# Batch 1's queries repacked by GpSimd and turned in 16 full transposes, with its second K^T V half and second scores one pair of products later

## Chip, cores, metric

One Trainium2 (trn2) chip, one core of it. The metric is the device time of one execution in microseconds (us); lower is better. Time before: 284.09 us, median of three runs (283.82 to 284.26).

## The reference, cut to what matters

```python
# q, k, v: [8 batches, 8 heads, 576 rows, 64]; w_in [512, 2048]; w_out [2048, 512]
kv  = einsum('bhsd,bhse->bhde', k, v)          # K^T V, one 64x64 matrix per head
out = einsum('bhsd,bhde->bhse', q, kv)         # "scores" below
x   = out / sqrt(mean(out**2, -1) + 1e-6) * g_norm
h   = x.reshape(4608, 512) @ w_in              # first product
y   = elu(h) @ w_out                           # second product
```

The kernel works in bf16 with float32 sums. It takes 512 rows of each batch in turn, and the 64 left over of each batch as a ninth group. TensorE writes its results to PSUM, its output memory; ACT and VectorE copy them from there to SBUF, where TensorE reads its operands. Such a copy is called an eviction here.

## The kernel before

The order of instructions on each engine is the order in the program. Batch 0 is done first. While its second product runs, TensorE also makes batch 1 ready: it transposes batch 1's q, forms K^T V and the scores in two halves `u`, and transposes the normalised rows, a half at a time.

```python
def q_t_single(q_pk, qt_ps, r, p):             # two 64-column transposes per 128 rows
    for j in range(J):
        for l in range(2):
            nc.tensor.transpose(
                qt_ps[l * 64 : l * 64 + 64, r, j * P : j * P + P],
                q_pk[:, 2 * p + l, j, :],
                ident,
            )

def q_t():
    qt_ps = at_tile(BF16).rearrange("p (r t) -> p r t", r=NPAIR)   # PSUM tile "at", one buffer
    ...
    for p in range(NPAIR):
        q_t_single(raw["q", T], qt_ps, p, p)
    nc.scalar.copy(qT[:, 0:2, :], qt_ps[:, 0:2, :])
    nc.scalar.copy(qT[:, 2:4, :], qt_ps[:, 2:4, :])
...
load_w_out(10, 12)                             # GpSimd issues these transfers
load_w_out(12, 14)
load_w_out(14, FC)
...
for j in range(J):
    mm2_quarter(0, j, 0)                       # second product of batch 0, rows 0..3 of w_out
    if j == 2:
        at["q"]()
for j in range(J):
    mm2_quarter(0, j, 1)
    if j == 1:
        at["kvu0"]()                           # first K^T V half
    if j == 2:
        at["seu0"](scores)                     # first scores, then square and sum
        at["sq0"]()
        at["sum0"]()
at["inv0"]()
at["mulu0"]()
for j in range(J):
    mm2(0, j, 8, 10)
    if j == 2:
        at["kvu1"]()                           # second K^T V half
at["seu1"]()                                   # second scores
at["sq1"]()
at["sum1"]()
for j in range(J):
    mm2(0, j, 10, 12)                          # rows 10 and 11 of w_out
    if j == 1:
        at["inv1"]()
        at["xu0"](scores[:, 0, :])             # first transposes of normalised rows
at["mulu1"]()
...
for j in range(J):
    mm2(0, j, 12, 14)
for j in range(J):
    mm2(0, j, 14, FC, hold=j > 1)
    if j == 0:
        at["xu1"](scores[:, 1, :])             # second transposes of normalised rows
```

`mm2(0, j, f0, f1)` issues one product of 128x512 for each row block `f` of w_out ("row" means such a block of 128). After this stretch the first product of batch 1 begins.

## Time and profile before

Two moments of TensorE: **S**, the start of batch 0's second product, and **E**, the start of batch 1's first product. What lies before S is called the head, and what lies between the first product on rows 10 and 11 and E the tail.

| kernel before, first trace | us |
|---|---|
| S | 28.31 |
| rows 10 and 11 of w_out land | 39.84 |
| first product on them starts | 39.97 |
| E | 46.06 |
| E - S, "the stretch" | 17.75 |

S and E are read from TensorE's timeline of the kernel before; columns are start, duration of the group, engine, source line, operation, output and inputs, shapes, count.

```profile
28.31 2.75 PE L514 MATMUL o_ps<-w_out_sb,gT 128*128 128x512 bf16 x12
...
39.63 0.41 PE L373 MATMUL at<-kv_sb,qT 64*128 64x64 bf16 x16
39.97 1.04 PE L514 MATMUL o_ps<-w_out_sb,gT 128*128 128x512 bf16 x4
...
46.06 1.89 PE L467 MATMUL at<-xT,w_in_sb 128*128 128x512 bf16 x8
```

From E on, TensorE is the bound, and each microsecond by which E moves is a microsecond of the result unless something later adds to it.

### The profile page before, as it was taken

Reading aid. Unit: us, or ns where it says so; the run is one execution under the profiler, and the core shown is the slowest. Engines: PE = TensorE matmul, PEld = TensorE weight load, DVE = VectorE, ACT = ScalarE, POOL = GpSimd, SP = SyncE. Lnnn points to the kernel's source line nnn. Section 1 sums busy time; section 2 is a strip of 40 time slices with the busy share of each in tenths; the row PEclk is TensorE's granted clock in tenths of the full one; section 3 lists DMA queues with packets and bytes.
Section 4 is the critical chain, followed back from the end, with each engine's and each line's share of the span. In section 5 each row is a group of like instructions: output and inputs, shape, how many; then the busy total and the mean of one; then the engine's idle time right before and its main releaser. Section 6 shows DMA issues by size and latency. Waiting matters only on the chain.

```text
span 282.0 us, 5163 instructions
## 1 busy us (share of the span) xinstructions
PE 276.0 (98%) x2134; PEld 129.8 (46%) x2134; DVE 159.8 (57%) x232; ACT 153.8 (55%) x221; POOL 56.2 (20%) x98
## 2 busy tenths in 40 slices
PE   7899999999999999999999999999999999999994
PEld 3444544445444444444444444444444444444444
DVE  2559453888388546843693469445854586444400
ACT  2679546666487438533863377337923692333311
POOL 7854422143421341004110421012000000000000
PEclk9999999999999999999999999999999999999999
DMA  7999999697796696359935795455236123010122
GB/s 196 199 200 202 208 201 191 179 170 128 178 177 114 157 157 156 74 149 121 198 78 148 95 211 73 130 114 148 55 94 76 77 38 112 0 77 0 74 76 74
DMA packets 57579, 35.98 MB, mean 128 GB/s; under 512 B 32852, under 2 KB 55124, under 8 KB 57556
## 3 DMA queue, kind: packets, MB, share of 16 engines
q0 software_dynamic: 21808, 17.30, 41.2%
q1 hardware_dynamic: 35348, 17.83, 24.7%
q10 hardware_dynamic: 400, 0.52, 0.6%
q8 instruction: 16, 0.26, 0.4%
q14 instruction: 7, 0.06, 0.1%
HBM read 36.70 MB, written 9.44 MB: 164 GB/s over the span
## 4 chain that ended last, share of the span: by engine, by line
PE 94%; DMA 2%; ACT 1%; DVE 0%; issue 0%; POOL 0%; POOLq 0%
PE h_ps L467 42%; PE o_ps L514 39%; PE o_ps L924 5%; DMA v_pk<-in_v_dram 2%; PE at L174 2%; PE at L467 1%; PE bank L684 1%; PE at L201 1%; PE h_ps L684 1%; PE se_ps L201 1%; ACT r L669 0%; ACT r L672 0%; PE at L185 0%; ACT sq L663 0%; PE se_ps L413 0%
## 5 line engine op out<-in xcount | busy, mean ns | idle before, releaser
L467 PE MATMUL h_ps<-xT,w_in_sb 128*128 128x512 bf16 x536 | 125.7, 379 | 0.0
L514 PE MATMUL o_ps<-w_out_sb,gT 128*128 128x512 bf16 x512 | 120.5, 379 | 0.0
L479 ACT ACTIVATE elu_e<-h_ps 128x1024 bf16<-128x1024 f32 (+1 forms) x71 | 70.0, 995 | 80.1 <-PE h_ps L467 78.5
L467 PEld LDWEIGHTS <-w_in_sb 128*128 128x128 bf16 x552 | 52.5, 98 | 63.3 <-DVE xT L333 1.7
L514 PEld LDWEIGHTS <-gT 128*128 128x128 bf16 x512 | 49.4, 98 | 58.4
L490 DVE TENSOR_SCALAR elu_e<-elu_e 128x1024 bf16<-128x1024 bf16 (+1 forms) x75 | 31.9, 425 | 73.4 <-ACT elu_e L479 73.4
L498 DVE TENSOR_TENSOR gT<-elu_e,h_ps 128x1024 bf16<-128x1024 bf16 (+1 forms) x51 | 60.1, 1179 | 5.3
L527 ACT COPY o_sb<-o_ps 128x512 f32<-128x512 f32 x32 | 18.6, 586 | 15.5 <-PE o_ps L514 15.5
L218 DVE TENSOR_REDUCE ss<-sq 128x16 f32<-128x1024 bf16 x16 | 19.4, 1218 | 11.1 <-ACT sq L213 10.4
L485 ACT ACTIVATE elu_h<-h_ps 128x1024 bf16<-128x1024 f32 (+1 forms) x20 | 19.5, 990 | 0.0
L150 POOL COPY q_bf<-q_pk 128x512 bf16<-128x512 bf16 x24 | 14.4, 629 | 24.3 <-DMA q_pk<-in_q_dram 24.3
L498 DVE TENSOR_TENSOR gT<-elu_e,elu_h 128x1024 bf16<-128x1024 bf16 x20 | 14.2, 709 | 2.5 <-ACT elu_h L485 1.0
L924 PE MATMUL o_ps<-w_out_sb,gT 128*128 128x512 bf16 (+1 forms) x80 | 14.1, 337 | 0.0
L125 POOL COPY gate<-qT 1x1 bf16<-1x1 bf16 x6 | 1.1, 181 | 58.4 <-DMA qT<-q_bf 58.4
L104 POOL DMA_DIRECT2D q_pk<-in_q_dram x14 | 10.6, 758 | 4.5 <-issue 1.5
L229 DVE TENSOR_TENSOR xs<-at,ss 128x512 bf16<-128x512 f32 x16 | 10.2, 682 | 1.2 <-ACT ss L225 1.2
L924 PEld LDWEIGHTS <-gT 128*128 128x128 bf16 x80 | 7.8, 98 | 6.4 <-DVE gT L498 0.4
L213 ACT ACTIVATE sq<-at 128x1024 bf16<-128x1024 f32 x9 | 9.4, 1043 | 1.6 <-PE at L201 1.0
L118 POOL DMA_DIRECT2D k_pk<-in_k_dram x12 | 8.3, 690 | 3.9 <-DMA w_in_sb<-in_moe_w_in_dram 2.4
L118 POOL DMA_DIRECT2D v_pk<-in_v_dram x12 | 8.2, 683 | 3.2 <-DMA w_out_sb<-in_moe_w_out_dram 1.8
L932 ACT COPY o_last<-o_ps 128x512 f32<-128x512 f32 (+1 forms) x5 | 2.5, 500 | 10.8 <-PE o_ps L924 10.8
L174 PEld LDWEIGHTS <-k_pk 64*64 64x64 bf16 x576 | 6.4, 107 | 4.3 <-issue 4.0
(79 smaller groups left out, 140.7 us busy)
## 6 DMA issues: line engine op xcount, KB each, us to landing
out_dram<-o_sb SPq DMA_DIRECT2D x16, 512.0 KB, 3.3
q_pk<-in_q_dram POOLq DMA_DIRECT2D x14, 256.0 KB, 5.7
k_pk<-in_k_dram POOLq DMA_DIRECT2D x6, 576.0 KB, 8.3
v_pk<-in_v_dram POOLq DMA_DIRECT2D x6, 576.0 KB, 11.6
w_in_sb<-in_moe_w_in_dram POOLq DMA_DIRECT2D x5, 256.0 KB, 7.4
st_q<-in_q_dram SPq DMA_DIRECT2D x2, 512.0 KB, 4.7
w_out_sb<-in_moe_w_out_dram POOLq DMA_DIRECT2D x2, 512.0 KB, 13.9
w_out_sb<-in_moe_w_out_dram POOLq DMA_DIRECT2D x4, 256.0 KB, 12.0
```

The costliest lines, as they stand in the source:

```text
L118: nc.gpsimd.dma_start(out=raw[name, b].rearrange("p h j d -> p h (j d)")[:, hs], in_=in_[:, hs])
L150: eng.tensor_copy(out=out_, in_=in_)
L174: nc.tensor.matmul(kv_ps[l * 64 : l * 64 + 64, s, u * 64 : u * 64 + 64], lhsT=bf["k", T][rows, j, 2 * u + l, :], rhs=bf["v", T][rows, j, 2 ...
L218: nc.vector.reduce_sum(out=ss, in_=sq.rearrange("p c (h e) -> p (c h) e", h=H), axis=AX.X)
L467: nc.tensor.matmul(h_ps[a][:, cs], lhsT=w_in_sb[:, c, f * P : f * P + P], rhs=x(c, cs), start=(c == 0), stop=(c == KC - 1),)
L479: nc.scalar.activation(e[:, lo:hi, :], ps, AF.Exp)
L485: nc.scalar.activation(h[:, lo:hi, :], ps, AF.Relu)
L490: nc.vector.tensor_scalar(out=e[:, lo:hi, :], in0=e[:, lo:hi, :], scalar1=1.0, scalar2=1.0, op0=ALU.min, op1=ALU.subtract,)
L498: nc.vector.tensor_tensor(out=gT[T][:, 2 * i + lo : 2 * i + hi, :], in0=e[:, lo:hi, :], in1=h, op=ALU.add if relu else ALU.max,)
L514: nc.tensor.matmul(o_ps[T, j], lhsT=gT[T][:, f, j * P : j * P + P], rhs=w_out_sb[:, f, :], start=(f == 0), stop=(f == FC - 1),)
L527: nc.scalar.copy(o_sb[T][:, j % 2, :], o_ps.pop((T, j)))
L924: nc.tensor.matmul(ps, lhsT=gT[B][:, f, j * P : j * P + P], rhs=w_out_sb[:, f, cols], start=(f == 0), stop=(f == FC - 1),)
```

## The change

Intent: let the idle GpSimd put two heads of q side by side, so that 16 full 128x128 transposes replace 32 half ones; share the eviction of q^T between ACT and VectorE; and give the second K^T V and scores their data with time in hand by placing them later. In the diff, `unpack_q` is the repack (four copies); `gated=False` leaves out its wait for v before the last copy.

```diff
-    def unpack_q(b, eng):
+    def unpack_q(b, eng, gated=True):
...
-            if j == J - 1:
+            if gated and j == J - 1:
                 after(bf["v", b][0:1, 0, 0, 0:1])
...
-    def q_t_single(q_pk, qt_ps, r, p):
+    def q_t_single(qb, qt_ps, p):
         for j in range(J):
-            for l in range(2):
-                nc.tensor.transpose(
-                    qt_ps[l * 64 : l * 64 + 64, r, j * P : j * P + P],
-                    q_pk[:, 2 * p + l, j, :],
-                    ident,
-                )
+            nc.tensor.transpose(
+                qt_ps[:, p, j * P : j * P + P],
+                qb[:, j, 2 * p : 2 * p + 2, :].rearrange("p h d -> p (h d)"),
+                ident,
+            )
...
-                q_t_single(raw["q", T], qt_ps, p, p)
+                q_t_single(bf["q", T], qt_ps, p)
             nc.scalar.copy(qT[:, 0:2, :], qt_ps[:, 0:2, :])
-            nc.scalar.copy(qT[:, 2:4, :], qt_ps[:, 2:4, :])
+            nc.vector.tensor_copy(out=qT[:, 2:4, :], in_=qt_ps[:, 2:4, :])
...
     load_w_out(10, 12)
+    unpack_q(1, Q, gated=False)
     load_w_out(12, 14)
...
         mm2_quarter(0, j, 0)
-        if j == 2:
-            at["q"]()
+    at["q"]()
...
         mm2(0, j, 8, 10)
-        if j == 2:
-            at["kvu1"]()
-    at["seu1"]()
-    at["sq1"]()
-    at["sum1"]()
+    at["kvu1"]()
     for j in range(J):
         mm2(0, j, 10, 12)
-        if j == 1:
+        if j == 0:
+            at["seu1"]()
+            at["sq1"]()
+            at["sum1"]()
+        if j == 2:
             at["inv1"]()
             at["xu0"](scores[:, 0, :])
```

## The prediction

> **What bounds the kernel now.** I read the page first, then the chain that ended last in order of time, then each engine's timeline from 28 to 46 us, where the diff acts.
>
> ```profile
> PE 276.0 (98%) x2134; PEld 129.8 (46%) x2134; DVE 159.8 (57%) x232; ACT 153.8 (55%) x221; POOL 56.2 (20%) x98
> PE 94%; DMA 2%; ACT 1%; DVE 0%; issue 0%; POOL 0%; POOLq 0%
> ```
>
> TensorE (PE) is busy 98% of the span and is 94% of the chain. After the head, a microsecond is saved only if PE does less, or waits less. Everything on the other engines is hidden until it makes PE wait. The chain in the affected stretch (start, us, what):
>
> ```profile
> 28.48 2.59 PE o_ps L514 x12
> 31.07 1.01 PE at L185 x32
> 32.08 2.70 PE o_ps L514 x12
> 34.77 0.41 PE at L174 x36
> ...
> 38.76 0.41 PE at L174 x36
> 39.16 0.54 PE o_ps L514 x2
> 39.70 0.34 PE at L373 x16
> 40.04 0.97 PE o_ps L514 x4
> 41.01 0.45 PE se_ps L413 x8
> 41.46 3.02 PE o_ps L514 x14
> 44.48 0.45 PE se_ps L413 x8
> ```
>
> L514 is the second product, L185 batch 1's half transposes of q, L174 its K^T V halves (the second at 38.76), L373 its scores (second at 39.70), L413 the turning of its normalised rows (halves at 41.01 and 44.48). From 47 us on the chain is product after product to 282; a delay of PE here has nothing to absorb it.
>
> Three lines of the timeline (start, us, engine, what, then idle and its end) and three answers of the DMA view, each for one issue alone (KB, us from issue to landing), give the slack:
>
> ```profile
> 39.31 0.25 ACT L352 CAST kv_sb<-at 128x128 bf16<-128x128 f32 x1
> 39.63 0.41 PE L373 MATMUL at<-kv_sb,qT 64*128 64x64 bf16 x16
> 42.98 1.29 DVE L391 TENSOR_TENSOR xs<-at,ss 128x512 bf16<-128x512 f32 x2 [0.62 <-ACT ss L225]
> ...
> q_pk<-in_q_dram POOLq DMA_DIRECT2D x1, 256.0 KB, 13.4
> v_pk<-in_v_dram POOLq DMA_DIRECT2D x1, 288.0 KB, 12.1
> w_out_sb<-in_moe_w_out_dram POOLq DMA_DIRECT2D x1, 256.0 KB, 12.1
> ```
>
> The last three are the issues at 15.40 (second half of q of batch 1: lands 28.8), 26.34 (last V heads of batch 1: 38.4) and 27.74 (rows 10 and 11 of w_out: **39.84**). The first product on those rows starts at 39.97 today: 0.13 us after they landed. That is the number I rest on.
>
> **What the Trainium skill says.** (1) "TensorEngine Tiling", Key Properties: changing the tiling mode drains TensorE. The trace agrees: full products start 0.216 us apart, and before each burst of half-array instructions the next start comes later than that by about 0.1 us (the transposes begin at 31.00 where the product before would have let go at 30.90; K^T V at 38.69 against 38.59). (2) "TensorE: Matmul & The Clock Gate", Wait — 56ns, not 53.3ns?: 55.6 ns start to start for 128 columns, 215.7 for 512. The trace agrees: the eight full transposes of L413 take 0.45 us. (3) "SBUF — State Buffer", Who interferes with whom: GpSimd and VectorE share a port pair, and the second to issue may block. GpSimd's existing repacks, same shape, took 604 to 813 ns, median 611, with VectorE busy beside several of them, so the price here is bounded. (4) "DMA: Bandwidth & Descriptors", Two DMAs through the same engine are not ordered: descriptors of one queue start in order. The landings of GpSimd's queue do come in order of issue, 1.2 to 1.6 us apart, at about 200 GB/s without a gap in this stretch.
>
> **The change part by part.**
>
> *Transposes.* 32 of 128x64 become 16 of 128x128. Old price: from 30.90 (next free slot) to 32.01 (first product after) = 1.11 us, mode switch included. New: 16 x 0.056 = 0.90, no switch. **-0.21 us**. The halves ran two at a time in the array's column halves, so halving the count gains little.
>
> *Repack.* Four GpSimd copies, starts 0.56 us apart, after q lands at 28.8 (GpSimd sees it about 29.0): 29.0 + 3 x 0.56 + 0.6 = 31.3. The transposes now stand after 16 products, not 12: 28.31 + 16 x 0.216 = 31.76, and only the fourth needs the last copy (31.93). Slack 0.4 to 0.6 us; no cost. The issue of w_out rows 12 and 13 slips from 29.06 to about 31.4, that of 14 and 15 from 31.55 to about 32.1; the fetch of batch 2's q at 33.01 waits for another landing (32.7) and stays. With up to eight transfers outstanding, the queue has work until 39.8, so order and landings should not move.
>
> *Evictions of q^T.* One of two ACT copies of 1.01 us becomes a VectorE copy; the head has the same shape at 0.69 us. Both finish by about 33.85 instead of 34.05. PE first needs them at 34.5 (slot of K^T V) either way: nothing on the path.
>
> *The move of K^T V and scores.* PE's ledger in the changed kernel, with 0.216 per product, 0.41 / 0.34 per burst and 0.1 per switch: transposes 31.76 to 32.66; 8 products to 34.39; first K^T V 34.48 to 34.89 (its V landed at 34.2); 4 products to 35.75; first scores to 36.19; 12 products to 38.78; second K^T V 38.88 to 39.28 (V landed 38.4). Then come two products on rows 10 and 11 **at 39.28**, before the second scores; today the scores (0.44 with their switch) and more stand before them. The rows land at 39.84, the queue of transfers does not know of PE's order, and PE should wait until about 39.9: **+0.6 us** of new wait, which swallows the 0.21 saved.
>
> *After that.* Two products to 40.33, second scores 40.43 to 40.77, 4 products 41.63, transposes 42.08, 12 products 44.66, then the second transposes. These wait for the chain scores, square, sum, inverse root, multiply. Today the scores start at 39.63 and the last multiply ends at 44.27 (42.98 + 1.29): 4.64 us. From 40.43 it ends at 45.07. Work between scores and these transposes was 18 products and 8 transposes; now it is 16 and 8, so 0.43 us of cover is gone, and today the fit was already within 0.1: the first four transposes need the first multiply (44.5, fits), the other four wait from 44.88 to about 45.2: **+0.3 us**. The stretch ends at 45.2 + 4 x 0.056 = 45.43, where it ended at 44.77 (44.32 + 8 x 0.056).
>
> Sum: 45.43 - 44.77 = +0.66 us, kept to the end. 284.09 + 0.66 = 284.75; I take **284.7**.
>
> **Rivals.**
> *A, the author's intent: the waits are all hidden.* If w_out rows land early enough and the multiplies too, 0.21 to 0.3 us is saved: 283.8. For it: the second K^T V gets 0.2 us more for its V, and the first half's turning moves away from its multiply (40.72 against a start at 40.85 today). Against it: 39.84 against 39.28.
> *B, no wait for w_out, but the multiply still late.* Scores then start at 39.82 (0.19 later), the multiply ends at 44.46, and the last four transposes wait 0.3 us; gain and wait cancel: 284.15. This is what comes out if the transfer lands 0.5 us earlier than in this one trace.
> *C, GpSimd late.* Copies at 0.81 us each end at about 32.2, PE waits another 0.3 us, or the w_out issues behind the repack slip so far that rows 12 and 13 (today 41.06, needed at about 42.5) arrive late. The first is absorbed by the wait at 39.9, so the time is still 284.7; the second would need over 1.4 us of slip in a queue that has ten microseconds of backlog: 285.5 at the outside.
>
> **Range and chances.** All rivals lie between 283.8 and 285.5, three tenths of a per cent on either side; three runs of the kernel before spread 0.44 us. 2% is 5.7 us, and PE's whole time in this stretch is 17. Predicted 284.7, 8 in 10 between 283.9 and 285.4. Faster by 2%: 0.5%, within 2%: 98.5%, slower: 1%.
>
> **What would show it.** Right: the 16 transposes take about 0.9 us and start right after 16 products; a PE gap of about 0.6 us ahead of the third pair of products after the second K^T V's slot, ended by a w_out transfer landing near 39.8; second scores near 40.4; a gap of some 0.3 us inside the second burst of row transposes. Wrong: no gap at 39.3 (rows landed earlier, rival B or A); a gap in the q transposes ended by GpSimd (C); gaps after 47 us, which I expect nowhere.

## The result, and the profile after

The first measurement gave 284.18 us (median of 4, 283.99 to 284.35) against 284.15 for the kernel before in the same rounds: ratio 1.0003, 95% interval 0.9985 to 1.0020. Ratios here are the mean time of one kernel's fast runs over that of the other's fast runs of the same rounds, so they are not quite the ratio of the medians. Ten runs of before and six of the changed kernel, later and on one chip, gave 284.22 against 283.78, ratio **1.0016** (1.0004 to 1.0029). The second says that the change costs about 0.45 us.

The engine shares and the chain of the changed kernel's first trace:

```profile
PE 273.5 (97%) x2088; PEld 129.3 (46%) x2118; DVE 161.7 (57%) x233; ACT 152.9 (54%) x220; POOL 59.7 (21%) x102
PE 89%; DMA 5%; ACT 2%; DVE 1%; issue 1%; POOL 1%; POOLq 0%
```

PE did not get shorter by 2.5 us: 30 matmul records are missing (2088 against 2118 weight loads), which the page warns of. Totals are useless for an effect of this size; starts of groups are not. TensorE in the stretch, first trace of the changed kernel:

```profile
28.65 3.62 PE L513 MATMUL o_ps<-w_out_sb,gT 128*128 128x512 bf16 x15
32.10 1.06 PE L184 MATMUL at<-ident,q_bf 128*128 128x128 bf16 x16
32.99 1.89 PE L513 MATMUL o_ps<-w_out_sb,gT 128*128 128x512 bf16 x8
34.98 0.48 PE L174 MATMUL at<-v_pk,k_pk 64*64 64x64 bf16 x36
...
39.40 0.48 PE L174 MATMUL at<-v_pk,k_pk 64*64 64x64 bf16 x36
39.81 0.39 PE L513 MATMUL o_ps<-w_out_sb,gT 128*128 128x512 bf16 x1
40.34 0.41 PE L372 MATMUL at<-kv_sb,qT 64*128 64x64 bf16 x16
...
44.71 0.72 PE L412 MATMUL se_ps<-ident,xs 128*128 128x128 bf16 x8
...
46.56 1.67 PE L466 MATMUL at<-xT,w_in_sb 128*128 128x512 bf16 x7
```

Four things are to be seen. The transposes take 32.10 to 32.99 = 0.89 us, and start after exactly 16 products (28.65 + 16 x 0.2157 = 32.10): no wait for GpSimd. The first K^T V starts at 34.98, where 32.99 + 8 x 0.2157 + 0.10 = 34.82 was free: 0.16 us lost. The products on rows 10 and 11 start at 39.81 with no wait. The second row transposes start at 44.71, where the 12 products ahead of them (from 42.00) let go at 44.59, and take 0.72 where eight unhindered ones show 0.61: 0.23 us lost. E is 46.56, half a microsecond later than in the trace of before; but S is also 0.34 later, so the stretch grew only from 17.75 to 17.91.

The 0.16 us has its cause on VectorE and ACT (timelines of the same trace; in brackets the idle time before and what ended it):

```profile
33.20 1.01 ACT L248 COPY qT<-at 128x1024 bf16<-128x1024 bf16 x1 [2.41 <-PE at L184]
34.24 0.69 DVE L249 COPY qT<-at 128x1024 bf16<-128x1024 bf16 x1 [2.46 <-ACT qT L248]
```

VectorE's half of the eviction waits for ACT's. They read two halves of one PSUM tile, and the program orders them one after the other. The tile is released at 34.93, and the first K^T V needs it at 34.82. The repack on GpSimd is done in time, in this line from 28.53 to 31.23, and the next fetches are issued right behind it:

```profile
28.53 2.70 POOL L150 COPY q_bf<-q_pk 128x512 bf16<-128x512 bf16 x4 [0.38 <-DMA q_pk<-in_q_dram]
31.18 1.40 POOL L142 DMA_DIRECT2D w_out_sb<-in_moe_w_out_dram  x2
```

The 0.23 us of the row transposes has two parts. The first of them starts 0.05 us after ACT's copy of the half before ends (44.66), the fifth waits for the second of VectorE's multiplies (44.98):

```profile
43.56 1.10 ACT L419 ACTIVATE xT<-se_ps,g_col 128x1024 bf16<-128x1024 bf16 x1
43.69 1.29 DVE L390 TENSOR_TENSOR xs<-at,ss 128x512 bf16<-128x512 f32 x2 [0.62 <-ACT ss L224]
```

So the wait on w_out, the centre of the prediction, was missing in this trace: the sign that the prediction itself had named for its rival A or B. Was it wrong, or was it hidden by the late S? That is the first question for the experiments.

### The profile page after: what moved, and what is told of

It is laid out like the page before. It is cut to its first block, busy times and chain, and to the rows that moved or that the text cites. A ratio compares the mean times of both kernels' runs of the same rounds, so it can differ in the third digit from the quotient of the medians.

```text
span 282.6 us, 5104 instructions
## 1 busy us (share of the span) xinstructions
PE 273.5 (97%) x2088; PEld 129.3 (46%) x2118; DVE 161.7 (57%) x233; ACT 152.9 (54%) x220; POOL 59.7 (21%) x102
## 4 chain that ended last, share of the span: by engine, by line
PE 89%; DMA 5%; ACT 2%; DVE 1%; issue 1%; POOL 1%; POOLq 0%
PE h_ps L466 40%; PE o_ps L513 37%; PE o_ps L923 5%; DMA w_in_sb<-in_moe_w_in_dram 3%; DMA k_pk<-in_k_dram 2%; PE at L174 2%; PE at L466 1%; PE at L200 1%; PE bank L683 1%; POOL w_in_sb L136 1%; PE se_ps L200 1%; DVE xs L228 0%; DVE ss L217 0%; PE se_ps L412 0%; ACT elu_e L478 0%
## 5 line engine op out<-in xcount | busy, mean ns | idle before, releaser
L513 PE MATMUL o_ps<-w_out_sb,gT 128*128 128x512 bf16 x488 | 118.2, 379 | 1.4 <-issue 0.3
L489 DVE TENSOR_SCALAR elu_e<-elu_e 128x1024 bf16<-128x1024 bf16 (+1 forms) x75 | 33.0, 440 | 73.2 <-ACT elu_e L478 73.2
L150 POOL COPY q_bf<-q_pk 128x512 bf16<-128x512 bf16 x28 | 18.0, 673 | 24.6 <-DMA q_pk<-in_q_dram 24.6
```

What stands on the lines that cost most here:

```text
L150: eng.tensor_copy(out=out_, in_=in_)
L489: nc.vector.tensor_scalar(out=e[:, lo:hi, :], in0=e[:, lo:hi, :], scalar1=1.0, scalar2=1.0, op0=ALU.min, op1=ALU.subtract,)
L513: nc.tensor.matmul(o_ps[T, j], lhsT=gT[T][:, f, j * P : j * P + P], rhs=w_out_sb[:, f, :], start=(f == 0), stop=(f == FC - 1),)
```

## The experiments

Theory: E is the later of two paths. On one, TensorE runs through from S. On the other, the first product on w_out rows 10 and 11 starts when they land (about 39.8 us; the DMA engines are busy without a gap in this stretch, at about 200 GB/s) and a fixed amount of work follows; the change lengthens that tail. Rivals: the change itself delays the head; the repack on GpSimd is what costs; the waits only hide others.

All traces in one table, with a granted clock of 0.997 or more. "First" is the first product on rows 10 and 11. In rows8 its record is missing; it is worked out as 0.53 before the second scores, the distance in the other kernels of that order. "Rest" is the time from E to the K^T V of batch 4 near 97 us.

| kernel | S | rows land | first | E | E - first | E - S | rest | ratio to before |
|---|---|---|---|---|---|---|---|---|
| before | 28.31 | 39.8 | 39.97 | 46.06 | 6.09 | 17.75 | 50.90 | |
| before_again | 28.69 | 39.8 | 40.35 | 46.43 | 6.08 | 17.74 | 50.80 | |
| only_repack | 28.43 | 39.6 | 40.03 | 46.12 | 6.09 | 17.69 | 50.79 | 0.9998 |
| repack_split | 28.85 | 40.1 | 40.28 | 46.36 | 6.08 | 17.51 | 51.16 | 1.0009 |
| best | 28.70 | 39.9 | 40.14 | 46.22 | 6.08 | 17.52 | 51.47 | 1.0014 |
| after | 28.65 | 39.7 | 39.81 | 46.56 | 6.75 | 17.91 | 51.01 | 1.0003 |
| after_again | 27.94 | 39.8 | 39.86 | 46.61 | 6.75 | 18.67 | 50.80 | |
| after_five | 28.44 | 39.9 | 39.96 | 46.71 | 6.75 | 18.27 | 50.80 | 1.0016 |
| split | 28.26 | 39.7 | 39.72 | 46.46 | 6.74 | 18.20 | 50.93 | 1.0030 |
| later | 28.06 | 39.8 | 39.84 | 46.36 | 6.52 | 18.30 | 51.01 | 1.0023 |
| only_move | 28.83 | 39.7 | 40.05 | 46.81 | 6.76 | 17.98 | 50.80 | 1.0020 |
| rows8 | 28.48 | not used | 39.65 | 46.40 | 6.75 | 17.92 | 50.80 | 1.0003 |
| rows_late | 28.86 | 41.0 | 41.09 | 47.84 | 6.75 | 18.98 | 50.80 | 1.0047 |
| repack_twice | 28.62 | 40.2 | 41.86 | 48.62 | 6.76 | 20.00 | 50.80 | 1.0077 |

### before_again and after_again: the same two kernels

> A second look at the kernel before, unchanged. The stretch is the time from the start of the first second product of batch 0 to the start of the first first-product of batch 1: 17.75 us in the first look (28.31 to 46.06). Theory 1: the start of the stretch is set by the landing of w_in in the head and moves by 0.3 us or so from look to look in either kernel, while the length of the stretch stays at 17.7 to 17.8. Theory 2: the change itself delays the head; then this look starts its stretch at 28.3 again within 0.05.

> A second look at the changed kernel. In the first look the stretch started at 28.65 and took 17.91 us. Theory 1 (head moves by chance): the start differs from 28.65 by 0.1 or more and the stretch grows when it starts earlier, because the landing of w_out rows 10 and 11 (39.74 in the first look) does not move with TensorE: with a start at 28.3 the first product on them waits about 0.2 us. Theory 2 (the change delays the head): start at 28.65 again, no wait.

Second look at the kernel before, TensorE's timeline:

```profile
17.45 0.82 PE L684 MATMUL bank<-xT,w_in_sb 128*128 128x512 bf16 x3 [0.54 <-DMA w_in_sb<-in_moe_w_in_dram]
...
28.69 2.75 PE L514 MATMUL o_ps<-w_out_sb,gT 128*128 128x512 bf16 x12
...
46.43 1.89 PE L467 MATMUL at<-xT,w_in_sb 128*128 128x512 bf16 x8
```

S moved from 28.31 to 28.69 in an unchanged kernel, with a wait for w_in in the head; the stretch stayed at 17.74. The changed kernel's S went the other way, from 28.65 to 27.94. The head moves by itself, so the rival that the change delays it falls. Second look at the changed kernel, the chain that ended last (start, us, what) and TensorE's timeline:

```profile
27.39 12.43 DMA w_out_sb<-in_moe_w_out_dram
39.82 0.04 issue
39.86 0.38 PE o_ps L513
```

```profile
27.94 3.62 PE L513 MATMUL o_ps<-w_out_sb,gT 128*128 128x512 bf16 x15
...
39.86 0.38 PE L513 MATMUL o_ps<-w_out_sb,gT 128*128 128x512 bf16 x1 [0.70 <-DMA w_out_sb<-in_moe_w_out_dram]
...
46.61 1.68 PE L466 MATMUL at<-xT,w_in_sb 128*128 128x512 bf16 x7
```

The predicted wait is there, 0.70 us, ended by the predicted transfer. TensorE was 0.71 us ahead of the first look, and E came out 0.05 later: the landing took it all.

### split: the two eviction copies from different PSUM tiles

```diff
-        def q_t():
+        def q_t(ps):
             qt_ps = at_tile(BF16).rearrange("p (r t) -> p r t", r=NPAIR)
+            qt_hi = ps.bitcast(BF16).rearrange("p (r t) -> p r t", r=2)
...
-                q_t_single(bf["q", T], qt_ps, p)
+                q_t_single(bf["q", T], qt_ps if p < 2 else qt_hi, p)
...
-            nc.vector.tensor_copy(out=qT[:, 2:4, :], in_=qt_ps[:, 2:4, :])
+            nc.vector.tensor_copy(out=qT[:, 2:4, :], in_=qt_hi)
...
-    at["q"]()
+    at["q"](scores[:, 0, :])
```

> The changed kernel with the second two head pairs of q transposed into another PSUM tile, so that VectorE's copy of them need not follow ACT's copy. Theory: the wait of 0.16 us ahead of the first K^T V goes, the first K^T V starts 0.1 to 0.2 us earlier counted from the start of the stretch (6.17 instead of 6.33), and TensorE now gets to w_out rows 10 and 11 before or as they land: if the stretch starts at 28.3, it waits 0.3 to 0.6 us there, as predicted; if at 28.65, 0 to 0.2. Stretch 17.75 to 18.3. Rival: the two copies still come one after the other (the rows of VectorE wait for ACT), stretch 17.9. Time within 0.1% of the kernel before.

```profile
32.36 1.01 ACT L249 COPY qT<-at 128x1024 bf16<-128x1024 bf16 x1 [1.96 <-PE at L184]
32.81 0.69 DVE L250 COPY qT<-se_ps 128x1024 bf16<-128x1024 bf16 x1 [1.41 <-PE se_ps L184]
...
34.43 0.48 PE L174 MATMUL at<-v_pk,k_pk 64*64 64x64 bf16 x36
...
39.72 0.38 PE L514 MATMUL o_ps<-w_out_sb,gT 128*128 128x512 bf16 x1 [0.41 <-DMA w_out_sb<-in_moe_w_out_dram]
```

The two copies now run side by side. The first K^T V starts 34.43 - 28.26 = 6.17 us after S, as expected (6.33 before the edit): the 0.16 is real and is the order of the two copies. It gains nothing, because TensorE then waits 0.41 for w_out. The expected time "within 0.1% of the kernel before" was a miss: ratio 1.0030 (1.0013 to 1.0046).

### later: the second row transposes one pair of products later

```diff
         mm2(0, j, 14, FC, hold=j > 1)
-        if j == 0:
+        if j == 1:
             at["xu1"](scores[:, 1, :])
```

> The changed kernel with the second burst of row transposes one product pair later (after the second of four of the last group, not the first). Theory: the 0.23 us by which that burst took longer (0.68 instead of 0.45, waiting for VectorE's last multiply) goes; stretch 17.91 - 0.23 = 17.68 if nothing else waits. Rival: that wait only hides another one (the copy with gain into x^T is then too late for the first product of batch 1), stretch 17.9. Time within 0.1% of the kernel before either way.

```profile
39.84 0.38 PE L513 MATMUL o_ps<-w_out_sb,gT 128*128 128x512 bf16 x1 [0.56 <-DMA w_out_sb<-in_moe_w_out_dram]
...
45.05 0.61 PE L412 MATMUL se_ps<-ident,xs 128*128 128x128 bf16 x8
```

The burst is back to 0.61, and E - first fell from 6.75 to 6.52: the waits in the burst were 0.23 us, and nothing took its place. The expected stretch of 17.68 was missed, since TensorE was early (S 28.06) and waited 0.56 for w_out. Time: ratio 1.0023 (1.0008 to 1.0038), a miss of the 0.1% as well, though the interval just reaches it.

### only_move and only_repack: each half of the change alone

only_move is the kernel before with the last hunk of the diff and nothing else; only_repack is the changed kernel with that hunk undone.

> The kernel before (half transposes straight from the packed q, both copies on ACT) with only the second K^T V half and second scores moved as in the change. Pinned theory: the first product on w_out rows 10 and 11 cannot start before about 39.8 us, and 6.7 us of work and waits stand after it, whatever TensorE saved before; so the first product of batch 1 starts at 46.5 to 46.7, as in the changed kernel (46.56 and 46.61), although 0.2 us more is done on the transposes, provided the stretch starts at or before 28.4. Rival (the changed kernel's extra time comes from the repack): 46.0 to 46.4 as in the kernel before. Time 0.1 to 0.3% above the kernel before.

> The changed kernel with the second K^T V half and second scores put back where they stood (scores ahead of the products on w_out rows 10 and 11). Pinned theory: those products again start when the rows land (39.7 to 39.8) or later, but only 6.1 us stand after them, so the first product of batch 1 starts at 45.9 to 46.1 with an early stretch (28.3 or before) and at the start of the stretch plus 17.6 to 17.75 with a late one. No wait inside the second burst of row transposes. Time 0.15 to 0.25% below the changed kernel's, equal to the kernel before within 0.1%. Rival (the repack on GpSimd is what costs): like the changed kernel, 46.5 or later.

only_move: S was late (28.83), so the condition of the expectation was not met and E came at 46.81 without a wait for w_out. It still tells the cost of the move without that wait: stretch 17.98 = 17.75 + 0.23, tail 6.76. Time: 284.24, ratio 1.0020 (1.0006 to 1.0034), as expected. The rival that the repack is what costs falls.

only_repack, the second scores and row transposes in TensorE's timeline:

```profile
39.69 0.41 PE L372 MATMUL at<-kv_sb,qT 64*128 64x64 bf16 x16
40.03 1.04 PE L513 MATMUL o_ps<-w_out_sb,gT 128*128 128x512 bf16 x4
...
44.37 0.61 PE L412 MATMUL se_ps<-ident,xs 128*128 128x128 bf16 x8
```

The scores stand ahead of rows 10 and 11 again, the tail is 6.09, no wait is left in the burst, and the time is that of the kernel before: 283.66 against 283.76, ratio 0.9998 (0.9985 to 1.0010). Its stretch, 17.69, is 17.75 - 0.22 for the transposes + 0.16 for the ordered copies.

### best and repack_split: what is good of it, put together

repack_split is only_repack with the edit of split; best is repack_split with the edit of later.

> As only_repack, with the two copies of q^T from separate PSUM tiles and the second burst of row transposes one pair of products later. Pinned theory: the landing at 39.7 to 39.8 still holds it, so no more than only_repack with an early stretch (45.9), 0.1 to 0.2 us better with a late one. Rival (each wait removed counts): 0.4 us below the kernel before, 0.14%. Time 0 to 0.15% below the kernel before.

> The changed kernel without the move (as only_repack), with the two copies of q^T from separate PSUM tiles. Theory: stretch 17.5 to 17.6 with a late start, as in the run called best, pinned to an end of 45.9 to 46.0 with an early one; time 0 to 0.15% below the kernel before and no worse than only_repack. If the repack of batch 4's q falls beside VectorE's work near 82 us again (start after 81 instead of near 80), 0.2 to 0.6 us are lost there, as in best.

Both stretches are as expected: 17.52 and 17.51, which is 17.75 less the 0.22 us of the transposes. The times show no gain: best 284.20, ratio 1.0014 (1.0001 to 1.0026), a miss; repack_split 283.77, ratio 1.0009 (0.9994 to 1.0023), which neither confirms nor excludes the small gain expected. Both traces have a late S, and both lose after E: their rest is 51.47 and 51.16 where most looks have 50.80. In best, GpSimd, VectorE and TensorE near 82 us:

```profile
81.44 2.38 POOL L150 COPY q_bf<-q_pk 128x512 bf16<-128x512 bf16 x3 [2.51 <-DMA q_pk<-in_q_dram]
81.60 0.74 DVE L490 TENSOR_SCALAR elu_e<-elu_e 128x1024 bf16<-128x1024 bf16 x1
83.27 0.83 DVE L490 TENSOR_SCALAR elu_e<-elu_e 128x1024 bf16<-128x1024 bf16 x1
85.48 1.89 PE L467 MATMUL h_ps<-xT,w_in_sb 128*128 128x512 bf16 x8 [0.33 <-DVE gT L498]
```

In the kernel before the same repack lies earlier, beside instructions that it does not hold up:

```profile
79.82 1.73 POOL L150 COPY q_bf<-q_pk 128x512 bf16<-128x512 bf16 x3 [2.54 <-DMA q_pk<-in_q_dram]
81.39 0.43 DVE L490 TENSOR_SCALAR elu_e<-elu_e 128x1024 bf16<-128x1024 bf16 x1
```

The repack of batch 4's q started when the data came, 1.6 us later, and it and VectorE lengthened each other (0.43 to 0.83 us, and 1.73 to 2.38 for three copies), until TensorE waited for VectorE (0.33 us at 85.48). That fits the lock on the shared port pair that the Trainium skill describes in "SBUF — State Buffer", Who interferes with whom; no experiment tested that cause. The same is in the first trace of the changed kernel, in split and in later (rest 50.93 to 51.01), but after_again, after_five, only_move and only_repack have a rest of 50.79 to 50.80. The meeting alone does not decide: repack_twice has it too, earlier (78.86 us, 2.38 for three copies), with a rest of 50.80. In repack_split the repack began at 83.40, after the VectorE instructions, which kept their 0.42. Its loss is another one: the first product at 93.97 could have started at 91.89 + 8 x 0.2157 = 93.62 but waited for VectorE, on a chain that runs through a DMA transposition of 9.60 us (x^T, issued at 81.74). That 0.35 us is nearly all of its excess over 50.80 (0.36). Why batch 4's q is sometimes fetched later is not settled here; it did not go with S or E in these traces.

### rows8: no wait for rows 10 and 11 (wrong result)

```diff
-                rhs=w_out_sb[:, f, :],
+                rhs=w_out_sb[:, f - 2 if T == 0 and f in (10, 11) else f, :],
```

> Wrong result on purpose: the changed kernel whose batch 0 multiplies with w_out rows 8 and 9 (long landed) where it should use rows 10 and 11, so that nothing waits for these; they are still fetched. Pinned theory: no wait after the second K^T V, the stretch is 17.9 us whatever its start (as in the first look of the changed kernel), so with a start at 28.0 to 28.3 the first product of batch 1 starts at 45.9 to 46.2, and the time falls by 0.1 to 0.25% against the changed kernel. Rival (the wait hides another that takes over, such as ACT's cast of the second K^T V or the multiply): 46.5 as before.

The trace is inconclusive: S was 28.48, TensorE reached the spot at 39.65, and a wait would have been 0.15 us at most. The stretch is 17.92 as expected. The times point the right way: four runs of 283.81 to 283.98, median 283.83, against 284.22 for the changed kernel in after_five, on the same chip. They were run at other times. Against the kernel before the ratio is 1.0003 (0.9988 to 1.0018); its interval overlaps that of after_five, so rows8 suggests and does not prove. rows_late is the firm test.

### after_five: the changed kernel with five rounds

> The changed kernel, unchanged, against the kernel before with five rounds on one chip. Theory: the kernel before is free to gain where its head is early (283.3 to 284.3 so far), the changed kernel is held at about 46.5 us by the landing of w_out rows 10 and 11 (284.0 to 284.5), so it is 0.1 to 0.25% slower: 0.3 to 0.7 us. The first product of batch 1 starts at 46.5 to 46.7 in the trace. Rival (they are equal, as the first result has it): within 0.05%.

E was 46.71 after a wait of 0.30 us for w_out (S 28.44). Median 284.22 (283.88 to 284.65) against 283.78 (283.42 to 284.20): ratio 1.0016 (1.0004 to 1.0029), as expected.

### rows_late: rows 10 and 11 land 1.2 us later

```diff
-    load_w_out(10, 12)
-    unpack_q(1, Q, gated=False)
     load_w_out(12, 14)
+    unpack_q(1, Q, gated=False)
+    load_w_out(10, 12)
```

> The changed kernel with the fetches of w_out rows 10, 11 and of 12, 13 exchanged, so that rows 10 and 11 land second (about 41.0 us). Pinned theory: the wait after the second K^T V grows, the first product on these rows starts at 41.0 to 41.1 whatever the start of the stretch, and the first product of batch 1 at 47.7 to 47.9; time 1.1 to 1.3 us above the changed kernel (0.4%). Rival (the wait is covered by the chain of the multiplies): 46.6 and no change in time.

```profile
41.09 0.38 PE L513 MATMUL o_ps<-w_out_sb,gT 128*128 128x512 bf16 x1 [1.00 <-DMA w_out_sb<-in_moe_w_out_dram]
...
47.84 1.89 PE L466 MATMUL at<-xT,w_in_sb 128*128 128x512 bf16 x8
```

The landing moved by 1.2 us and E moved with it, to the 47.84 that the theory gives. Time: 285.23, ratio 1.0047 (1.0032 to 1.0062), 1.0 us above the changed kernel and a little under the expected 1.1 to 1.3.

### repack_twice: the repack made twice

```diff
-            copy_on(eng, bf["q", b][:, j], t[:, :, j])
+            for _ in range(1 if gated else 2):
+                copy_on(eng, bf["q", b][:, j], t[:, :, j])
```

> The changed kernel with each of batch 1's four repack copies made twice. Theory: GpSimd ends at about 33.4 instead of 31.2; TensorE waits in the first four transposes until then (over 1 us), the slack of the single repack being 0.9 us or so; transposes end near 34.2, the first product of batch 1 starts at 47.6 to 47.9, and no wait remains at w_out rows 10 and 11; time 1.0 to 1.3 us above the changed kernel. w_out rows 12 to 15, issued after the repack, still land by 42.3. Rival: the late fetches behind the repack arrive late and cost more, 48.5 or later.

```profile
28.55 5.70 POOL L151 COPY q_bf<-q_pk 128x512 bf16<-128x512 bf16 x8 [0.38 <-DMA q_pk<-in_q_dram]
34.31 0.90 PE L185 MATMUL at<-ident,q_bf 128*128 128x128 bf16 x13 [1.00 <-POOL q_bf L151]
```

The mechanism is as expected, the size is not: the eight copies took 5.70 us, 0.71 each instead of 0.6, E was 48.62 instead of 47.6 to 47.9, and the time 285.91, 1.7 us up. E lies where the rival had put it, but not for the rival's reason: the fetches behind the repack, issued three microseconds late, still landed before they were needed, and the tail is 6.76 as in the other kernels with the move. The whole delay stands in the first four transposes: the fourth starts at 34.31, where it could have at 32.08 + 3 x 0.056 = 32.25. So the single repack does lie free, with about 0.9 us to spare in the first trace (its end at 31.2 against the fourth transpose at 32.3, less the signal) and about 0.5 in after_again, where S is earliest (30.97 against 31.56).

## Why the prediction was right or wrong

The time came out 0.5 us under the 284.7 said, well inside 283.9 to 285.4. The mechanism predicted exists, but the first trace did not show it: there the wait for w_out was 0, and a late S stood in for it. It showed in the other two traces of the changed kernel, and rows_late shows that the landing is its cause. By the prediction's own steps:

- **Transposes, -0.21:** right. 0.89 us against 0.90 said, and 17.75 - 17.51 = 0.24, 17.75 - 17.52 = 0.23 for the kernels that have nothing else of the change on the path.
- **Repack, no cost:** right, with the fetches behind it unhurt (repack_twice).
- **Evictions, nothing on the path:** wrong. "Both finish by about 33.85" took the two copies as parallel. They are ordered, the tile came free 0.16 us too late for the first K^T V, and split shows it.
- **Wait for rows 10 and 11, +0.6:** the right transfer, but not a constant. It was 0, 0.30 and 0.70 us in three traces of the changed kernel, because S moves between 27.94 and 28.86 over all looks while the landing stays near 39.8 (39.6 to 40.2, rows_late apart). I had S from one trace. Even there the +0.6 was too much: at S = 28.31 TensorE is free at 28.31 + (39.81 - 28.65) = 39.47, so the wait would be about 0.4, because the 0.16 lost on the copies comes off it.
- **Second row transposes, +0.3:** right in size; 0.23, shown by later and by only_move. About half of it stands ahead of the first transpose, which I had said would fit: I had not counted ACT's copy, which shares their PSUM tile.
- **The end of the stretch:** the predicted 45.43 for the end of the burst gives E = 45.43 + 6 x 0.2157 = 46.72. Measured: 46.56, 46.61, 46.71. In after_again and after_five the sum was good because the landing decides and not what TensorE did before it. In the first trace that is luck: S was 0.34 late, and TensorE came to the rows just after they had landed.
- **The time, 284.7:** 0.5 too high. The term that failed is the base. The difference of 0.66 is against a trace with S at 28.31, from an execution of 283.72 us, and I added it to the median of other executions, 284.09. Added to its own execution it gives 284.38; the profiled execution of the changed kernel took 284.35, by the luck just told. The difference itself is not a constant either. An estimate from the two paths: at S = 28.31 the changed kernel has E = 39.84 + 6.75 = 46.59, 0.53 after the kernel before; at S = 28.69, as in before_again, it has E = 28.69 + 17.91 = 46.60, only 0.17 after it. Measured were +0.03 us in the first rounds and +0.45 in six runs against ten, not 0.66. The runs of the kernel before span 283.31 to 284.26.

In one line: without a wait for w_out the change is -0.22 + 0.16 + 0.23 = +0.17 us (measured: 17.91 - 17.75 = 0.16), and with an early head TensorE waits up to 0.70 for the landing. The kernel before would meet that landing too, but with a tail of 6.09 and so only below E = 39.84 + 6.09 = 45.93 (an estimate; none of its traces came that early). Rival B of the prediction, no wait for w_out but a late multiply, 284.15, is the first trace, except for the ordered copies; the first 284.18 alone could not tell it from the prediction. Where the expected gain went: into a late multiply, an ordered pair of copies, and a landing. No version was shown to beat the kernel before, and none with rows 10 and 11 fetched earlier was tried.

## What to carry to other kernels

Before moving work of the bounding engine, list the landing times of everything that the instructions behind it read: what stands ahead of a landing is free as long as TensorE still comes early to it, and what is moved behind it is paid in full (here 0.44 us of scores and the chain behind them). Half-width transposes that run two at a time were nearly as good as full ones here (1.01 us against 0.89, and 0.10 for the switch), so the price of making them full (here the ordered copies, 0.16 us, and the multiply that came late, 0.23) was more than the gain. And compare a predicted difference with the execution that the trace came from, not with the median of others; if the head of a kernel moves by more than the effect, take several traces and compare stretches, not spans.

## What the Trainium skill lacked or had wrong

- "TensorEngine Tiling (Array Packing)", Key Properties, says that a change of mode drains TensorE but gives no price. Here it is about 0.10 us ahead of a burst (second K^T V of the kernel before: 38.69 against a free slot at 38.59).
- "TensorE: Matmul & The Clock Gate", Part 4: PE-mode transpose, gives some 275 to 390 ns for a 128x128 bf16 transpose. In a burst here they start 0.056 us apart: 16 in 0.89 us. The section has nothing on bursts: that transposes follow each other as closely as other products of 128 columns. Nor has it anything on the 32 half transposes, which took 1.01 us two at a time.
- "DMA: Bandwidth & Descriptors", Anatomy of one DMA — SWDGE (gpsimd) path, has a fit that gives 2.6 us for 256 KB. With the queue kept full, 256 KB (rows 10 and 11) took 11.9 to 12.7 us from issue to landing here; the page has no figure for a queue with transfers ahead. In repack_twice rows 12 to 15, issued 3 us late, took only about 6.9 us: the landing followed the bytes ahead of it.
- "SBUF — State Buffer", Who interferes with whom, agrees in kind: VectorE's instruction went from 0.43 to 0.74 and 0.83 us, and three GpSimd copies from 1.73 to 2.38, where they met; that the lock is the cause is not shown. No page says how such a meeting reaches TensorE: in best the rest was 51.47 us instead of 50.80, with a wait of 0.33 for VectorE in it, and in repack_twice nothing was lost.
- No page has the moving head: S varied by 0.9 us over fourteen traces of kernels with the same head.
